# A chunked scan with an MLP behind it: decay loads, the order of the opening and the place of the long scan are changed

## Chip, core and metric

The kernel runs on one core of one Trainium2 chip. The core has a matrix engine (PE, its weight loads are shown as PEld), a vector engine (DVE), a scalar engine (ACT), GpSimd (POOL) and a queue engine (SyncE, SP) which here only issues DMAs; ACT can issue DMAs too. Each engine runs its own instructions in the order in which they were written. The metric is the device time of one execution in microseconds; less is better.

## What is computed

```python
log_a = np.log(np.clip(a, 1e-06, 1.0))
for c in range(nc):                       # chunks of the sequence
    cum = np.cumsum(la, axis=-1)
    L = np.exp(cum[..., :, None] - cum[..., None, :]) * causal
    y_intra = einsum('bhij,bhjd->bhid', einsum('bhin,bhjn->bhij', Cc, Bc) * L, xc)
    y_inter = einsum('bhin,bhnd->bhid', Cc, state) * exp(cum)
    state = exp(sum(la)) * state + sum_j Bc_j xc_j exp(cum_end - cum_j)
x = y.transpose(0, 2, 1, 3).reshape(3072, 256)
h = x @ w_in                              # 256 -> 2048
out = gelu_tanh(h) @ w_out                # 2048 -> 256
```

There are 4 batches of 8 heads with 768 tokens, 32 values a head and a state of 16; x, a, B and C come in as fp32, and so do the weights (2 MB each).

## The kernel before

The kernel takes chunks of 128 tokens, 6 to a batch, and works on **pairs** of chunks: pair u is 256 tokens, 12 pairs in all. Decays are never taken as logarithms: a backward running product of a (a scan on DVE) gives each token's decay to the end of its chunk, which scales B, and its reciprocal scales C. Steps are named by a letter and indices, and the names below are those of the order table.

- **Short decays**: `load_aq` brings the decays of chunks 0 to 3 of all batches as 128 rows of 128 into `aq_t`; `clipq`, `Rq` (scan, L331), `tpq` (32x32 turns, L342), `recip0` and `peq` follow on DVE. `mulb` and `mulc` (L416, L409) scale B and C of chunks 0 to 3 of batch 0, `tw` turns them on PE, `ew` copies them out of PSUM into `bh` and `ce`.
- **Long decays**: `load_a` brings all decays as 64 rows of 384 into `a_t`; `clip`, `R` (scan of 384, L331), `tp2`, `tp6` (turns), `recip1`, `recip`. Chunks 4 and 5 of batch 0 (pair 2) need `tp2`, `recip1`, `mul1`, `T1` (PE turns), `ce1`, `bh1`, `N1`, `bn1`; later batches need `tp6` and `recip`. `pe` and `pp` make `pend`, the decays of whole chunks.
- **A pair**: `G` (L595) makes the products of C and B in the PSUM tiles ga and gb, `M` (L605) masks them with the triangle on DVE. For pair 0 alone the half gb goes another way: `GE` copies it on ACT, `ME` (L616) masks it on POOL. `XX` and `XD` bring x of chunks 0 to 3 into rows and make the chunk's state, `S` (L676) carries the state on, `SP` (L683) spreads it. `Y` (L650, L659) makes y in PSUM tile yb, `yev` copies it to `xm`.
- **The MLP of a pair**: `s1.u.i` (L709, i from 0 to 7, four matmuls each) into one of two PSUM tiles hp, `gelu.u.i` on ACT, and `s2.u.k.q` (L727, four matmuls each, quarter q of w_out for chunk k) into PSUM tile o_ps; `oev` copies that out and `store` writes it. s1.u.0 and 1 need quarter 0 of w_in, 2 and 3 quarter 1, and so on.
- **Weights**: `load_wi.q` and `load_wo.q` bring a quarter (512 KB, fp32) each, `wi.q.k` and `wo.q.k` cast one half of a quarter to bf16 on POOL, DVE or ACT as the table says (L316, L318, L314).
- **Fillers**: `~n` stands for matmuls of zeros, n blocks of 128 columns, which keep PE running while it has nothing else.

Nothing is planned at run time. The string `ORDERED` lists every step; it is walked once, and each engine gets its instructions in that order (a letter behind the colon chooses the engine, A for ACT, D for DVE, P for POOL, S for SP). A step that waits holds everything that stands behind it on its engine. All loads but three go through SP's queue: two of the four `load_aq` and one `load_a` are issued by ACT.

Of the kernel before, what the change touches and what calls it, by code (L numbers as in the profile page):

```python
# [19 lines left out]
c_wz c_ident c_zero c_unp load_aq.2:A load_bc0.1 c_tri load_aq.1:S load_aq.3:S load_aq.0:A c_m8  # L20
c_sel c_warm c_m4 load_bc0.0 load_x4 clipq Rq tpq load_a.0:A load_a.1:S peq ~53 ppq pendq:A
load_wi.0 c_cz c_bmask recip0 mulc.0:D mulc.1:D mulb:P ~9 tw.1 tw.0 ew.0.0:D c_par ew.0.1:A tw.2
ew.0.2:A x4.1:D ~8 G.0 clip ew.1.0:A ew.1.1:A load_wi.1 M.0.0 GE.3 x4.0:P GE.2 load_wi.2 ~2 XX.0
XD.0 load_wo.0 xn.0:A ew.1.2:A SP.0 S.0.0 xn.1:A wi.0.0:A wi.0.1:A R ~13 G.1 S.0.1 load_wi.3 XX.1
load_bc1.0 xn.2:A ME.3:P ME.2:P pe Y.0 XD.1 pp yev.0.0.2:A S.1.0 load_wo.1 load_bc1.1 SP.1 S.1.1
load_wo.2 wi.1.1:P M.1.0 wi.2.0:P wo.0.0:D pend:A wo.0.1:P wi.2.1:P SP.2 wi.1.0:A M.1.1 s1.0.0
gelu.0.0 s1.0.1 gelu.0.1 xn.3:A wi.3.1:P s1.0.2+4 gelu.0.2 s1.0.3 s2.0.0.0.o load_wo.3 wo.1.0:P
gelu.0.3 load_bc.1.0 s1.0.4 wi.3.0:A s1.0.5 gelu.0.4 Y.1 tp2 mul1.0 gelu.0.5 yev.1.0.2:A s1.0.6
s1.0.7 gelu.0.6 load_x.2 tp6.0 load_bc.1.1 load_x.3 gelu.0.7 recip1 T1.0 s2.0.1.0.o s1.1.0 bh1:D N1
s1.1.1 wo.1.1:A tp6.3 s2.0.0.1.o wo.2.1:P gelu.1.0 gelu.1.1 mul1.1 tp6.2 T1.1 tp6.1 ce1.1:A ce1.0:A  # L30
wo.2.0:A bn1:D recip.1.4 s2.0.1.1.o s1.1.2 s1.1.3 gelu.1.2 wo.3.0:A wo.3.1:P G.2 gelu.1.3 s2.0.0.2.o
s2.0.1.2.o s2.0.0.3.o castx.2.None:P s2.0.1.3.o load_bc.2.1 M.2.0 mul.1.0 M.2.1 oev.1:A s1.1.4
s1.1.5 T.1.0 load_x.4 oev.0:A s2.1.0.0.o castx.3.None:P s2.1.0.1.o gelu.1.4 SP.3 D.2 gelu.1.5 s1.1.6
S.2.0 SP.4 load_x.5 E.1.0:A N.1 mul.1.1 bn.1:D gelu.1.6 s1.1.7 Y.2 s2.1.0.2.o T.1.1 gelu.1.7
yev.2.0.2:A s1.2.0 s1.2.1 gelu.2.0 E.1.1:D F.1 s2.1.0.3.o s1.2.2 gelu.2.1 gelu.2.2 D.3 load_bc.2.0
oev.2:D G.3 S.3.0 S.3.1 s2.1.1.0.o load_x.6 castx.4.None:P s1.2.3 gelu.2.3 s2.1.1.1.o s2.1.1.2.o
s1.2.4 M.3.1 M.3.0 gelu.2.4 SP.6 s2.1.1.3.o s1.2.5 oev.3:A gelu.2.5 D.4 Y.3 mul.2.1 S.4.0 G.4 s1.2.6
s2.2.0.0.o SP.7 castx.5.None:A yev.3.0.2:A gelu.2.6 S.4.1 s1.2.7 mul.2.0 s2.2.0.1.o s1.3.0
s2.2.0.2.o gelu.2.7 M.4.0 M.4.1 load_x.8 store_s.2.1 gelu.3.0 s1.3.1 s2.2.0.3.o s1.3.2 G.5 gelu.3.1
SP.8 gelu.3.2 store_s.2.0 D.5 Y.4 M.5.1 oev.4:A S.5.0 s1.3.3 s2.2.1.0.o s2.2.1.1.o gelu.3.3 s1.3.4  # L40
s1.3.5 s2.2.1.2.o yev.4.0.2:D s2.2.1.3.o SP.9 SP.10 gelu.3.4 gelu.3.5 s1.3.6 oev.5:A turn_s.2.1
s1.3.7 gelu.3.6 store.1 s2.3.0.0.o M.5.0 gelu.3.7 s2.3.0.1.o store.4 load_s.2 turn_s.2.0 load_x.7
# [23 lines left out]
gelu.10.3 s1.10.4 s1.10.5 oev.18:A gelu.10.4 s2.9.1.0.o s2.9.1.1.o gelu.10.5 s1.10.6 store.13
s1.10.7 s2.9.1.2.o s2.9.1.3.o gelu.10.6 gelu.10.7 s1.11.0 oev.19:A gelu.11.0 s1.11.1 s2.10.0.1.yb
s2.10.0.2.yb s2.10.0.3.yb gelu.11.1 oev.20:A store.20 store.18 s1.11.2 gelu.11.2 s1.11.3 s2.10.1.0.o
gelu.11.3 s2.10.1.1.o s1.11.4 s1.11.5 gelu.11.4 gelu.11.5 s2.10.1.2.o s2.11.0.0.yb s1.11.6 s1.11.7
gelu.11.6 s2.10.1.3.o s2.11.0.1.yb oev.21:D store.21 gelu.11.7 s2.11.0.2.yb s2.11.0.3.yb oev.22:A  # L70
store.22 store.19 s2.11.1.0.o s2.11.1.1.o s2.11.1.2.o s2.11.1.3.o oev.23:A store.23
# [891 lines left out]
```

## Time and profile before

| | us |
|---|---|
| runs | 116.67, 116.80, 116.95; median 116.8 |
| profiled execution, span (first to last instruction) | 115.1 |
| median less span, what lies around it | 1.7 |
| PE busy | 109.4 (95% of the span) |
| ACT busy | 75.1 (65%) |
| DVE busy | 68.7 (60%) |
| POOL busy | 15.1 (13%) |

The page gives no other time of the profiled execution than its span. Times in the views are microseconds from the start of the span. A row of the timeline reads: start, time from its start to the end of its last instruction, engine, line, operation, what is written and read, shapes, count, and in brackets the idle time of the engine just ahead with what ended it. Instructions of one engine overlap by some hundredths to tenths of a microsecond, so a duration is a little longer than the step from one start to the next.

### The profile page before, as it was taken

Reading aid. Unit: us, or ns where it says so; the run is one execution under the profiler, and the core shown is the slowest. Engines: PE = TensorE matmul, PEld = TensorE weight load, DVE = VectorE, ACT = ScalarE, POOL = GpSimd, SP = SyncE. Lnnn points to the kernel's source line nnn. Section 1 sums busy time; section 2 is a strip of 40 time slices with the busy share of each in tenths; the row PEclk is TensorE's granted clock in tenths of the full one; section 3 lists DMA queues with packets and bytes.
Section 4 is the critical chain, followed back from the end, with each engine's and each line's share of the span. In section 5 each row is a group of like instructions: output and inputs, shape, how many; then the busy total and the mean of one; then the engine's idle time right before and its main releaser. Section 6 shows DMA issues by size and latency. Waiting matters only on the chain.

```text
span 115.1 us, 3372 instructions
## 1 busy us (share of the span) xinstructions
PE 109.4 (95%) x1425; PEld 92.2 (80%) x1425; DVE 68.7 (60%) x135; ACT 75.1 (65%) x149; POOL 15.1 (13%) x32
## 2 busy tenths in 40 slices
PE   6999799999999999999999999999999999999990
PEld 2354578978877979799898998998989989999970
DVE  6688799998799989196966281546827421000100
ACT  3119889978657767657576486377766765685710
POOL 6564274122220000020002000000000000000000
PEclk9999999999999999999999999999999999999999
DMA  2999999949969828959478760000014014001132
GB/s 65 236 280 286 397 293 311 278 84 218 225 109 226 214 64 203 192 147 265 102 158 184 174 178 0 6 0 0 0 50 138 0 49 139 0 0 51 46 103 79
DMA packets 43006, 15.97 MB, mean 139 GB/s; under 512 B 36656, under 2 KB 41456, under 8 KB 42992
## 3 DMA queue, kind: packets, MB, share of 16 engines
q1 hardware_dynamic: 42848, 15.68, 53.9%
q8 instruction: 11, 0.18, 0.6%
q10 hardware_dynamic: 144, 0.08, 0.4%
q14 instruction: 3, 0.02, 0.1%
HBM read 11.04 MB, written 3.93 MB: 130 GB/s over the span
## 4 chain that ended last, share of the span: by engine, by line
PE 82%; DMA 8%; SPq 4%; POOL 1%; issue 1%; ACT 0%
PE hp L709 36%; PE o_ps L727 33%; DMA wf<-in_moe_w_out_dram 8%; PE yb L727 3%; PE ga L595 3%; PE yb L650 2%; PE yb L659 2%; SPq L190 1%; PE hp L628 1%; SPq L162 1%; SPq L159 1%; SPq L150 1%; POOL w_out_sb L316 1%; POOL w_in_sb L316 1%; SPq L183 1%
## 5 line engine op out<-in xcount | busy, mean ns | idle before, releaser
L713 ACT ACTIVATE gT<-hp 128x512 bf16<-128x512 f32 x96 | 53.3, 595 | 24.5 <-PE hp L709 24.0
L709 PE MATMUL hp<-xm,w_in_sb 128*128 128x256 bf16 x384 | 51.9, 273 | 0.5 <-ACT pend L314 0.3
L727 PE MATMUL o_ps<-w_out_sb,gT 128*128 128x256 bf16 x352 | 46.4, 273 | 0.0
L709 PEld LDWEIGHTS <-w_in_sb 128*128 128x128 bf16 x384 | 41.2, 114 | 3.2 <-issue 1.7
L727 PEld LDWEIGHTS <-gT 128*128 128x128 bf16 x384 | 37.0, 98 | 4.7 <-issue 0.8
L318 DVE COPY o_sb<-o_ps 128x256 f32<-128x256 f32 x7 | 3.0, 424 | 22.4 <-PE o_ps L727 18.4
L605 DVE TENSOR_TENSOR m<-ga,tri 128x1024 bf16<-128x1024 f32 x12 | 14.6, 1216 | 0.0
L605 DVE TENSOR_TENSOR m<-gb,tri 128x1024 bf16<-128x1024 f32 x11 | 13.4, 1219 | 0.5 <-PE gb L595 0.5
L697 PE MATMUL yb<-wz 128*128 128x512 bf16 (+2 forms) x24 | 8.2, 491 | 1.1 <-DVE warm L222 1.1
L314 ACT ACTIVATE o_sb<-o_ps 128x256 f32<-128x256 f32 x15 | 5.6, 382 | 4.1 <-PE o_ps L727 3.0
L683 DVE SCALAR_TENSOR_TENSOR sp_new<-s_new,pend,bmask 128x256 bf16<-128x256 f32 x17 | 8.0, 479 | 0.1
L316 POOL CAST x<-x_t 128x512 bf16<-128x512 f32 x5 | 3.2, 648 | 34.9 <-DMA x_t<-in_x_dram 22.9
L676 DVE SCALAR_TENSOR_TENSOR s_new<-s_new,pend,hp 128x64 f32<-128x64 f32 x13 | 3.6, 279 | 5.7 <-PE hp L628 5.5
L697 PEld LDWEIGHTS <-wz 128*128 128x128 bf16 x25 | 2.9, 126 | 5.0 <-issue 3.6
L659 PE MATMUL yb<-m,x 128*32 128x128 bf16 x192 | 6.1, 219 | 0.0
L650 PE MATMUL yb<-ce,sp_new 128*32 128x128 bf16 x160 | 5.3, 220 | 0.0
L595 PE MATMUL ga<-ce,bh 32*128 32x256 bf16 x48 | 4.7, 272 | 0.1
L314 ACT ACTIVATE xm<-yb 128x512 bf16<-128x512 f32 x8 | 4.8, 597 | 0.0
L595 PE MATMUL gb<-ce,bh 32*128 32x256 bf16 x48 | 4.7, 273 | 0.0
L727 PE MATMUL yb<-w_out_sb,gT 128*128 128x256 bf16 x32 | 4.1, 273 | 0.0
L659 PEld LDWEIGHTS <-x 128*32 128x32 bf16 x192 | 3.8, 97 | 0.4 <-issue 0.2
L650 PEld LDWEIGHTS <-sp_new 128*32 128x32 bf16 x160 | 3.0, 96 | 1.0 <-issue 1.0
(108 smaller groups left out, 78.4 us busy)
## 6 DMA issues: line engine op xcount, KB each, us to landing
out_dram<-o_sb SPq DMA_DIRECT2D x24, 128.0 KB, 2.0
x_t<-in_x_dram SPq DMA_DIRECT2D x20, 128.0 KB, 3.8
wf<-in_moe_w_in_dram SPq DMA_DIRECT2D x4, 512.0 KB, 8.3
wf<-in_moe_w_out_dram SPq DMA_DIRECT2D x4, 512.0 KB, 8.9
bc_t<-in_B_dram SPq DMA_DIRECT2D x3, 384.0 KB, 4.8
bc_t<-in_C_dram SPq DMA_DIRECT2D x3, 384.0 KB, 4.3
scr<-bc SPq DMA_DIRECT2D x4, 192.0 KB, 3.1
x_t<-in_x_dram SPq DMA_DIRECT2D x1, 512.0 KB, 4.8
```

The source lines that it names most:

```text
L314: nc.scalar.activation(o, i, AF.Copy)
L316: nc.gpsimd.tensor_copy(out=o, in_=i)
L595: nc.tensor.matmul(out=gbank(g)[:, 256 * k:256 * k + 256], lhsT=bh_of(2 * u + k)[gs], rhs=ce_of(2 * u + k)[gs], start=True, stop=True, til ...
L605: nc.vector.tensor_tensor(out=m_of(u)[:, 2 * i:2 * i + 2].rearrange("p g k e t -> p (g k e) t"), in0=gx[i].rearrange("p g (k t) -> p (g k) ...
L650: nc.tensor.matmul(out=y4[32 * j:32 * j + 32, k, w], lhsT=sp[:, 32 * h:32 * h + 32], rhs=ce_of(gc)[:, h % 2], start=first(j), stop=False, ...
L659: nc.tensor.matmul(out=y4[32 * j:32 * j + 32, k, w], lhsT=X16[u][:, k, 32 * h:32 * h + 32], rhs=m[:, h // 2, h % 2, :], start=first(j), st ...
L676: nc.vector.scalar_tensor_tensor(out=s_new, in0=state[("s", gc - 1)], scalar=pend_of(gc), in1=d, op0=ALU.mult, op1=ALU.add)
L683: nc.vector.scalar_tensor_tensor(out=sp_new.rearrange("p (g d) -> p g d", g=4), in0=(XN[0][:, H * D:H * D + 64] if gc == 0 else state[("s" ...
L697: nc.tensor.matmul(out=t[:, 0:m * 128], lhsT=wz, rhs=w3.to_broadcast([128, m, 128]), start=True, stop=True, skip_group_check=True)
L709: nc.tensor.matmul(out=hp[:, j * T:(j + 1) * T], lhsT=w_in_k[:, w, q, k], rhs=xm[:, w, u * T:(u + 1) * T], start=(w == 0), stop=(w == 1))
L713: nc.scalar.activation(gts[u][:, 2 * i:2 * i + 2], hps.pop((u, i)).rearrange("p (j t) -> p j t", j=2), AF.Gelu_apprx_tanh)
L727: nc.tensor.matmul(out=ops[gc], lhsT=gts[u][:, fi, k * Q:(k + 1) * Q], rhs=w_out_sb[:, fi, :], start=(fi == 0 and (u > 0 or k == 0)), stop ...
```

## The change

Loads: the four loads of the short decays become one, of 128 rows, first on SP (rows of other batches than 0, of which nothing is used later, now hold other values). B comes ahead of C, x directly behind C, then quarter 0 of w_in and the two loads of the long decays, all on SP. Quarter 0 of w_out comes ahead of quarter 2 of w_in.

```diff
-    def load_aq(i, eng):
-        (nc.scalar if eng == "ACT" else nc.sync).dma_start(out=aq_t[32 * i:32 * i + 32], in_=a_rows(i * Q, Q))
+    def load_aq(eng):
+        (nc.scalar if eng == "ACT" else nc.sync).dma_start(
+            out=aq_t, in_=bass.AP(tensor=a.tensor, offset=a.offset, ap=[[P4, 16], [S, H], [1, Q]]))
...
-    aq = [add("A", load_aq, i, alt="AS") for i in range(R4)]
+    aq = [add("S", load_aq, alt="S")]
```

The order of SP's first loads before (aq_t short decays, a_t long decays, bcf B and C, x_t x, wf a quarter of a weight):

```order
L150 DMA bcf_100<-in_C_dram 128x8x64
L159 DMA aq_t<-in_a_dram 32x128 x2
L150 DMA bcf_100<-in_B_dram 128x8x64
L183 DMA x_t<-in_x_dram 128x8x128
L162 DMA a_t<-in_a_dram 32x384
L190 DMA wf<-in_moe_w_in_dram 128x2x512 x3
L194 DMA wf<-in_moe_w_out_dram 128x1024
L190 DMA wf<-in_moe_w_in_dram 128x2x512
```

and of the change:

```order
L161 DMA aq_t<-in_a_dram 128x1x128
L152 DMA bcf_100<-in_B_dram 128x8x64
L152 DMA bcf_100<-in_C_dram 128x8x64
L186 DMA x_t<-in_x_dram 128x8x128
L193 DMA wf<-in_moe_w_in_dram 128x2x512
L165 DMA a_t<-in_a_dram 32x384 x2
L193 DMA wf<-in_moe_w_in_dram 128x2x512
L197 DMA wf<-in_moe_w_out_dram 128x1024
L193 DMA wf<-in_moe_w_in_dram 128x2x512 x2
```

x moved up by one place and the first weight quarter by two, and the quarters of w_in and w_out alternate differently. Further down, the x of pairs 3 and 4 and the store of chunk 0 now stand ahead of B and C of batch 2; the loads behind them keep their order.

Opening: the zero fill of `cz` moves from POOL to ACT, that of `unp` from DVE to POOL, and four copies into `unp` become one.

```diff
+        nc.scalar.activation(cz.rearrange("p e r h n -> p (e r) (h n)"),
+                             wz.rearrange("p (o n) -> p o n", o=1).to_broadcast([128, 2 * R4, H * N]), AF.Copy)
...
-        for r in range(R4):
-            nc.vector.tensor_copy(out=unp[:, r, :, r], in_=sub)
+        nc.vector.tensor_copy(out=diag, in_=sub.rearrange("p (o q) -> p o q", o=1).to_broadcast([128, R4, P4]))
```

The masks: pair 1 now goes the way of pair 0, so half of its mask leaves DVE for ACT and POOL. `s1.1.0` no longer depends on the last s1 of pair 0 (in the table it still stands directly behind it). An unused form of `SP` for POOL is added, and a single small matmul, `gate`, which waits for `tpq`.

```diff
+GEU = (0, 1)
...
-        if u:
+        if u not in GEU:
...
-                s.deps.append(s1.get((u - 1, NI - 1)))
+                s.deps.append(s1.get((u - 1, NI - 1)) if u > 1 else None)
...
+        elif w == "gate":
+            nc.tensor.matmul(out=yb[0:4, 0:1], lhsT=rt0[0][:, 0, 0:4], rhs=rt0[0][:, 0, 0:1],
+                             start=True, stop=True, skip_group_check=True)
```

The table: its first third is new, and from F.1 (batch 1) on it is nearly the old one. Two of its lines, before and after:

```diff
-S.0.0 xn.1:A wi.0.0:A wi.0.1:A R ~13 G.1 S.0.1 load_wi.3 XX.1
+wo.0.1:P wi.2.0:D wo.0.0:D clip R Y.1 yev.1.0.2:A s1.0.3 gelu.0.3 wi.2.1:P tp2
```

On DVE the place between the first masks and the turns of the long decays was this (r_t is the long scan, w_out_sb the cast of a weight half, m masks, sp_new and s_new states, pe the chunk decays):

```order
L331 SCALAR_TENSOR_TENSOR r_t<-ac,ends 64x384
L676 SCALAR_TENSOR_TENSOR s_new<-s_new,pendq,hp 128x64
L385 TENSOR_TENSOR pe_111<-ac,r_t 64x3
L387 TENSOR_TENSOR pe_112<-pe_111,m_117 64x24
L676 SCALAR_TENSOR_TENSOR s_new<-s_new,pendq,hp 128x64
L683 SCALAR_TENSOR_TENSOR sp_new<-s_new,pendq,bmask 128x256
L676 SCALAR_TENSOR_TENSOR s_new<-s_new,pendq,o_ps 128x64
L605 TENSOR_TENSOR m<-ga,tri 128x1024
L318 CAST w_out_sb<-wf 128x512
L683 SCALAR_TENSOR_TENSOR sp_new<-s_new,pendq,bmask 128x256
L605 TENSOR_TENSOR m<-gb,tri 128x1024
L342 STREAM_TRANSPOSE rt_126<-r_t 32x64 x4
```

and is now this, from pair 1's states on (bc0s is `mul1`; the two instructions of `ce1` come next):

```order
L329 CAST w_in_sb<-wf 128x512
L329 CAST w_out_sb<-wf 128x512
L339 TENSOR_SCALAR ac<-a_t 64x384
L342 SCALAR_TENSOR_TENSOR r_t<-ac,ends 64x384
L353 STREAM_TRANSPOSE rt_126<-r_t 32x64 x4
L353 STREAM_TRANSPOSE rt<-r_t 32x192 x2
L385 RECIPROCAL pt_128<-rt_126 128x16
L353 STREAM_TRANSPOSE rt<-r_t 32x192
L446 TENSOR_TENSOR bc0s_134<-bcf_101,pt_128 128x256
L446 TENSOR_TENSOR bc0s_134<-bcf_101,rt_126 128x256
L396 TENSOR_TENSOR pe_111<-ac,r_t 64x3
L398 TENSOR_TENSOR pe_112<-pe_111,m_117 64x24
```

The clip and the long scan now stand behind the casts of two weight halves (quarter 2 of w_in, quarter 0 of w_out). Before the turns the second half of pair 1's mask is gone from DVE; behind them `ce1` and one more weight cast have come from ACT and POOL, and `bh1` and `bn1` have gone to ACT.

On POOL the casts and masks after pair 0's mask read before:

```order
L616 AFFINE_SELECT m<-ge_140 128x512 x2
L316 CAST w_in_sb<-wf 128x512 x2
L316 CAST w_out_sb<-wf 128x512
L316 CAST w_in_sb<-wf 128x512 x2
L316 CAST w_out_sb<-wf 128x512 x3
```

and now:

```order
L627 AFFINE_SELECT m<-ge_140 128x512 x2
L327 CAST w_in_sb<-wf 128x512 x4
L627 AFFINE_SELECT m<-ge_141 128x512 x2
L327 CAST w_out_sb<-wf 128x512
L327 CAST w_in_sb<-wf 128x512 x3
L327 CAST w_out_sb<-wf 128x512 x4
```

POOL has 16 instructions here in place of 10: three more halves of w_in, one more of w_out, and pair 1's mask. The last two of the row x4 are both halves of quarter 3 of w_out, of which ACT had one before.

More of the change, by code (lines that the diff above doesn't have):

```diff
@@ L18 @@
 SCR = (2, 3)
+GEU = (0, 1)
 ORDERED = """
[L20 to L42, printed above, removed]
@@ L66 @@
[L66 to L71, printed above, removed]
+c_wz c_ident c_unp0:P c_bmask c_tri c_m8 c_sel c_m4 c_zero load_aq load_bc0.0 load_bc0.1 load_x4
@@ L226, in c_zero, with c_unp0 @@
         nc.vector.memset(ac[:, HS:HS + 1], 0.0)
-        nc.vector.memset(unp, 0.0)
+    def c_unp0(eng):
+        (nc.gpsimd if eng == "POOL" else nc.vector).memset(unp, 0.0)
     def c_warm():
@@ L297 @@
     xm = const.tile([128, 2, n_tokens], BF16, name="xm")
+    spf = [const.tile([128, 64], FP32, name=f"spf{i}") for i in range(2)]
     gx = [ps1.tile([128, 2, 512], FP32, name=f"g{i}") for i in "ab"]
@@ L679, in f_S, with f_SP @@
         state[("s", gc)] = s_new
-    def f_SP(gc):
+    def f_SP(gc, eng):
         sp_new = st.tile([128, 256], BF16, name="sp_new")
+        if eng == "POOL":
+            sc = spf[gc % 2]
+            nc.gpsimd.tensor_scalar(out=sc, in0=state[("s", gc)], scalar1=pend_of(gc + 1), scalar2=None, op0=ALU.mult)
+            nc.gpsimd.tensor_tensor(out=sp_new.rearrange("p (g d) -> p g d", g=4),
+                                    in0=sc.rearrange("p (o d) -> p o d", o=1).to_broadcast([128, 4, 64]),
+                                    in1=bmask.rearrange("p (g d) -> p g d", g=4), op=ALU.mult)
+            state[("sp", gc)] = sp_new
+            return
         nc.vector.scalar_tensor_tensor(
```

115 lines of the change are left out of this document (75 added, 40 removed).

## The prediction

> **What bounds the kernel now.** I read the chain of waits first: the page's shares of it by engine, then its pieces in order of time (start, length, engine and what is written).
>
> ```profile
> PE 82%; DMA 8%; SPq 4%; POOL 1%; issue 1%; ACT 0%
> ```
>
> ```profile
> 6.23 9.55 DMA wf<-in_moe_w_out_dram
> 15.83 0.87 POOL w_out_sb L316
> 16.70 0.76 POOL w_in_sb L316
> 17.51 0.96 PE hp L709 x7
> ...
> 112.11 0.38 ACT o_sb L314
> ```
>
> The program has two parts. From 17.51 to 112.11 PE is the chain and never pauses; behind it come one copy and one store. Ahead of 17.51 the chain is a weight load, its cast on POOL, and a second cast that stood behind it there. The second part is the same work in both kernels, in nearly the same order. So the time changes by how much earlier or later PE has done the same work at a place where both kernels have come together again, unless PE pauses after it. I take two such places from PE's timeline (start, length, engine, line, op, written and read, shapes, count):
>
> ```profile
> 14.18 1.03 PE L709 MATMUL hp<-xm,w_in_sb 128*128 128x256 bf16 x8 [0.28 <-ACT pend L314]
> ...
> 20.84 0.28 PE L463 MATMUL ga<-ident,bh 128*128 128x128 bf16 x2
> 20.95 0.60 PE L709 MATMUL hp<-xm,w_in_sb 128*128 128x256 bf16 x4
> 21.39 0.60 PE L727 MATMUL o_ps<-w_out_sb,gT 128*128 128x256 bf16 x4
> ...
> 23.67 1.92 PE L727 MATMUL o_ps<-w_out_sb,gT 128*128 128x256 bf16 x16
> ...
> 29.08 0.29 PE L650 MATMUL yb<-ce,sp_new 128*32 128x128 bf16 x8
> ```
>
> Four matmuls of an s1 or s2 take 0.44 (20.95 to 21.39), so 0.11 each. N1, two turns, takes 0.11 (20.84 to 20.95), so N.1, six turns, about 0.34. Place one is the end of pair 0's s2: 23.67 + 1.92 = 25.59. Ahead of it stand in both kernels all of pair 0, the first four s1 of pair 1, Y.1, T1 and G.2; only N1 follows it now instead. Place two is the start of Y.2, 29.08. The change has everything ahead of it but N.1, so being level there means 29.08 - 0.34 = 28.74.
>
> What holds PE up to these places are the weights. A cast that waited for a load shows when the load landed (ACT, then POOL):
>
> ```profile
> 11.78 1.15 ACT L314 ACTIVATE w_in_sb<-wf 128x512 bf16<-128x512 f32 x2 [0.19 <-DMA wf<-in_moe_w_in_dram]
> ...
> 23.87 0.63 ACT L314 ACTIVATE w_out_sb<-wf 128x512 bf16<-128x512 f32 x1
> ```
>
> ```profile
> 10.22 1.22 POOL L616 TENSOR_SCALAR_AFFINE_SELECT m<-ge 128x512 bf16<-128x512 bf16 x2 [1.71 <-ACT ge L610]
> 13.16 0.61 POOL L316 CAST w_in_sb<-wf 128x512 bf16<-128x512 f32 x1 [1.72 <-DMA wf<-in_moe_w_in_dram]
> ...
> 15.83 0.87 POOL L316 CAST w_out_sb<-wf 128x512 bf16<-128x512 f32 x1 [0.71 <-DMA wf<-in_moe_w_out_dram]
> ```
>
> Quarter 0 of w_in landed at 11.78, quarter 1 at 13.16, quarter 0 of w_out at 15.8, quarter 3 of w_out by 23.87. The last had its halves cast side by side on ACT and POOL, until 24.5. PE needs it for the last eight of the sixteen matmuls of 23.67, at about 24.6. It comes just in time: an earlier weight alone wins nothing here, a later one is paid in full.
>
> **The change: loads.** SP's timeline, then two stretches of one microsecond (PE, PEld, DVE, ACT, POOL busy, clock, DMA share, GB/s):
>
> ```profile
> 0.80 0.46 SPq L150 DMA_DIRECT2D bcf<-in_C_dram  x1
> 1.32 1.03 SPq L159 DMA_DIRECT2D aq_t<-in_a_dram  x2
> 2.39 0.42 SPq L150 DMA_DIRECT2D bcf<-in_B_dram  x1
> 2.86 0.58 SPq L183 DMA_DIRECT2D x_t<-in_x_dram  x1
> ```
>
> ```profile
> 3.00:4.00 1.00, 1.00 (x3) 0.29 (x2) 0.96 (x3) 0.23 (x2) 0.93 (x3) 1.00 0.89 174
> 23.00:24.00 1.00, 1.00 (x15) 0.57 (x14) 1.00 (x3) 1.00 (x3) 0.33 (x2) 1.00 0.20 40
> ```
>
> The bytes ahead of each landing are the same as before, with quarter 0 of w_out and quarter 2 of w_in (512 KB each) in exchanged places. So a quarter lands earlier only by what the stream starts earlier or runs denser. x was issued at 2.86. Now one short load (about 0.5, half of 1.03), B and C (0.42 and 0.46) stand ahead of it: 0.80 + 0.5 + 0.42 + 0.46 = 2.18, some 0.7 sooner. On the other side the first issue stays at 0.80, so the first byte comes no sooner, which makes nothing the lower end. Call the advance d. It lies between 0 and 0.7, and I take **d = 0.5**: nearer the upper end, since the weak stretch from 3 to 4 (174 GB/s), when small decay loads ran between C and B, should fill.
>
> **The short decays.** DVE's timeline, with the rows of the later parts too:
>
> ```profile
> 5.16 0.23 DVE L328 TENSOR_SCALAR acq<-aq_t 128x128 f32<-128x128 f32 x1 [0.89 <-DMA aq_t<-in_a_dram]
> ...
> 11.60 0.94 DVE L331 TENSOR_TENSOR_SCAN r_t<-ac,ends 64x384 f32<-64x384 f32 x1
> ...
> 15.80 0.43 DVE L318 CAST w_out_sb<-wf 128x512 bf16<-128x512 f32 x1
> 16.14 0.83 DVE L683 SCALAR_TENSOR_TENSOR sp_new<-s_new,pendq,bmask 128x256 bf16<-128x256 f32 x1
> ...
> 18.14 0.99 DVE L342 STREAM_TRANSPOSE rt<-r_t 32x64 f32<-32x64 f32 x4
> ...
> 28.18 0.48 DVE L683 SCALAR_TENSOR_TENSOR sp_new<-s_new,pend,bmask 128x256 bf16<-128x256 f32 x1
> ```
>
> DVE waited for the four loads until 5.16; the last of them was issued in the second half of 1.32 + 1.03, so it took some 3.2. One load issued at 0.80 should be there between 3 and 4, and the opening starts 1 to 2 earlier. What is late next is C, now third in the queue, and then quarter 0 of w_in: POOL casts both halves, 11.78 - d + 2 x 0.61 = 12.5, and PE's first s1 starts there instead of at 14.18. **These 1.7 are not in the sum**: PE meets the later weights anyway and spends them waiting.
>
> **Bound one, the last weight.** Quarter 3 of w_out lands at 23.87 - d. Both its halves now stand on POOL, one behind the other: 23.87 - d + 2 x 0.61 = 25.09 - d. Two of four matmuls of this s2 can run after the first half; two of it and four of its sister remain, 6 x 0.11 = 0.66. Place one is reached at 25.75 - d, and N1 (0.11) is still to come. Against 25.59 that is 0.27 - d; with d = 0.5 a **gain of 0.23**.
>
> **Bound two, DVE with the long scan late.** Quarter 2 of w_in lands where quarter 0 of w_out did, at 15.80 - d. Behind its cast on DVE stand a second cast (0.43 each), the clip of 384 (0.23 for 128 at 5.16; I take 0.35) and the scan, 0.94: 2.15, and 2.0 after overlaps. From the turns to the end of the last state spread ahead of Y.2 DVE took 28.18 + 0.48 - 18.14 = 10.5. Out of that stretch go the copies `bh1` and `bn1` to ACT; in come two of `ce1`, one cast of 0.43 and two tiny products of `pe`. The trace has `ce1` on ACT alone: between nothing more than the two copies and three casts more, 0 to 1.3; I take 0.5, one cast and the products, so 11.0. Y.2 can start at 15.80 - d + 2.0 + 11.0 = 28.8 - d; level is 28.74. Alone that would be a gain of 0.44 at d = 0.5, so bound one ends last, by 0.2.
>
> **Edits taken at nothing.** Pair 1's mask on POOL follows quarter 1's casts, 13.16 - d + 4 x 0.61 = 15.1. Y.1, which needs it, stood behind the group of 17.51 before, so it is free as long as POOL is less than 2 late; after that each microsecond is paid. The zero fill of `cz` on ACT, 1.2 by two halves of 1.15: ACT has nothing else until PE's first product, and if that cover went, mulc would wait. `unp` and the fillers lie ahead of the first s1, in the 1.7 that the sum leaves out; so does `gate`, behind which on PE only fillers and the first turns wait. The early store on SP waits for chunk 0's copy, just behind place one, and holds B and C of batch 2 and the x of pair 5; these are first used well behind 28.18, and a hold longer than that distance would be paid in full.
>
> **Rivals.** *The casts and DVE hinder each other* (slower). DVE cast from 15.80 and POOL from 15.83: POOL's cast took 0.87 in place of 0.61, and DVE's next spread, at 16.14 over the same cast, 0.83 in place of the 0.48 at 28.18. A meeting cost DVE 0.35 and POOL 0.26. The scan at 11.60 met nothing, since POOL stood still from 10.22 + 1.22 = 11.44 to 13.16. Now it runs, with two casts and the clip, while POOL has six casts nearly in a row: up to four meetings. DVE's bound becomes 28.8 - d + 0.35 k; from k = 1 it ends last, and with k = 3 it is 29.35, which against 28.74 is 0.6 slower: **117.4**. Against it: POOL also waits for landings in that stretch, so not each pair meets.
>
> [...]
>
> *The stream is not earlier*, d near 0.1. Then POOL's two casts in series are paid: 0.27 - 0.1 = 0.17 slower, **117.0**. For it speaks that the bytes are the same and the first issue too; against it x's earlier issue.
>
> *The stream is earlier by more*, d near 1. From 23 to 24 the DMA engines were 0.20 busy at 40 GB/s, while the last quarter was released only at 23.87: a few of the sixteen engines were late with their share. If they are not late again, both bounds move with d: 0.27 - 1.0 is a gain of 0.73, **116.0**. Against it: nothing in the change touches how a load is shared out.
>
> **How the numbers follow.** The median of the runs, 116.8, stands 1.7 above the span of 115.1; the shifts apply to both, so the forecast is 116.8 - 0.23 = **116.6**. A difference under about 0.2%, 0.23 us, can't be told from none. Chances: forecast 0.36, hindering 0.28, stream not earlier 0.16, stream much earlier 0.20. The forecast sits on the bound: 0.20 of its 0.36 go to faster, 0.16 to same. Hindering gives 0.26 slower and 0.02 same, the stream not earlier 0.05 slower and 0.11 same, the early stream 0.20 faster. Together faster 0.40, same 0.29, slower 0.31. The range reaches from a little beyond the early stream, 115.7, to three meetings with d a little smaller, 117.6.
>
> **What would show it.** Right: the first s1 at about 12.5, then pauses of PE in several places up to 24; quarter 3 of w_out released at about 23.4 with PE waiting for its second half; the spread ahead of Y.2 done by 28.3; no pause of PE behind that. Wrong: the scan or a cast longer by 0.3 than in these rows, Y.2 waiting for DVE, a pause of PE after Y.2, or weights released at times other than about 0.5 earlier.

## The result, and the profile after

The changed kernel took 118.73 us (median of 118.10, 118.63, 118.83, 119.36) beside 116.88 for the kernel before in the same round: a ratio of 1.0154, 95% interval 1.0113 to 1.0195. It is **slower by 1.5%**, 1.8 us. 116.6 was predicted, with a range from 115.7 to 117.6. Every ratio here leaves out executions that took over about 1.5% longer than the fastest of their kernel. The profiled execution has a span of 117.0, and its time was 118.83.

The chain of waits by engine (the page's line), and its longest pieces ahead of PE's part in order of time:

```profile
PE 78%; DMA 8%; SPq 5%; DVE 4%; issue 1%; ACT 0%
```

```profile
2.80 1.16 SPq L186
6.92 9.18 DMA wf<-in_moe_w_in_dram
17.60 1.34 DVE r_t L342
```

DVE, which had no share worth a name, now has 4%, and its longest piece is the long scan `r_t`. PE's timeline (start, length, ..., and in brackets its idle time with what ended it):

```profile
12.34 0.63 PE L728 MATMUL hp<-xm,w_in_sb 128*128 128x256 bf16 x4
...
16.61 0.30 PE L728 MATMUL hp<-xm,w_in_sb 128*128 128x256 bf16 x1 [0.59 <-DVE w_in_sb L329]
17.08 0.52 PE L728 MATMUL hp<-xm,w_in_sb 128*128 128x256 bf16 x3 [0.17 <-POOL w_in_sb L327]
...
19.39 1.06 PE L728 MATMUL hp<-xm,w_in_sb 128*128 128x256 bf16 x8 [0.49 <-POOL w_in_sb L327]
...
22.38 0.28 PE L454 MATMUL gb<-ident,bc0s 128*128 128x128 bf16 x2 [0.64 <-DVE bc0s L446]
...
24.02 0.28 PE L606 MATMUL ga<-ce,bh 32*128 32x256 bf16 x2
...
24.89 0.40 PE L404 MATMUL hp<-pe,selp 64*128 64x24 f32 x2
...
26.10 1.04 PE L746 MATMUL o_ps<-w_out_sb,gT 128*128 128x256 bf16 x8
...
30.40 0.30 PE L661 MATMUL yb<-ce,sp_new 128*32 128x128 bf16 x8
```

The first s1 starts at 12.34, 1.84 sooner than before. Then PE waits 0.76 for quarter 2 of w_in, 0.49 for quarter 3, and 0.64 at `T1.1` (22.38) for `mul1.1` on DVE. From there it doesn't pause. Place one, the end of pair 0's s2, is 26.10 + 1.04 = 27.14 in place of 25.59, and place two, the start of Y.2, is 30.40 in place of the level 28.74: 1.66 late. PE's last group of 16 matmuls is 1.65 late too (111.81 for 110.16), so nothing is lost in between; the rest of the 1.9 by which the span is longer lies behind PE's last matmul.

Most of the 1.66 was lost ahead of T1.1. In the kernel before, T1.0 and T1.1 started at 21.82; without T1.0 (0.11), N1 (0.11) and the one s1 (0.44) that no longer stand ahead of it, level there is 21.16, and 22.38 is 1.22 late. Another 0.33 is `pp`, the two fp32 matmuls at 24.89 (the step that follows starts at 25.22). In the kernel before it had stood ahead of the first s1:

```profile
13.49 0.40 PE L393 MATMUL hp<-pe,selp 64*128 64x24 f32 x2
```

It needs the long scan. With the scan late it had to move into the stretch in which PE never pauses, and there its time is paid. DVE and POOL ahead of T1.1 and up to Y.2:

```profile
16.12 0.43 DVE L329 CAST w_in_sb<-wf 128x512 bf16<-128x512 f32 x1 [1.15 <-DMA wf<-in_moe_w_in_dram]
16.46 0.83 DVE L329 CAST w_out_sb<-wf 128x512 bf16<-128x512 f32 x1
17.22 0.34 DVE L339 TENSOR_SCALAR ac<-a_t 64x384 f32<-64x384 f32 x1
17.60 1.33 DVE L342 TENSOR_TENSOR_SCAN r_t<-ac,ends 64x384 f32<-64x384 f32 x1
18.96 2.08 DVE L353 STREAM_TRANSPOSE rt<-r_t 32x64 f32<-32x64 f32 x6
...
21.89 0.43 DVE L446 TENSOR_TENSOR bc0s<-bcf,pt 128x256 bf16<-128x256 f32 x1
...
29.53 0.28 DVE L687 SCALAR_TENSOR_TENSOR s_new<-s_new,pend,hp 128x64 f32<-128x64 f32 x1 [0.47 <-PE hp L639]
29.84 0.48 DVE L702 SCALAR_TENSOR_TENSOR sp_new<-s_new,pend,bmask 128x256 bf16<-128x256 f32 x1
```

```profile
16.15 0.87 POOL L327 CAST w_in_sb<-wf 128x512 bf16<-128x512 f32 x1 [0.65 <-DMA wf<-in_moe_w_in_dram]
17.51 1.83 POOL L327 CAST w_in_sb<-wf 128x512 bf16<-128x512 f32 x2 [0.49 <-DMA wf<-in_moe_w_in_dram]
...
23.37 1.37 POOL L327 CAST w_out_sb<-wf 128x512 bf16<-128x512 f32 x2 [2.92 <-DMA wf<-in_moe_w_out_dram]
```

DVE waits 1.15 for quarter 2, which is there at 16.1. Then each thing that PE needs next, `T1.1` first, stands behind two casts, the clip and the scan. One cast took 0.83 for 0.43 and the scan 1.33 for 0.94, both beside a cast on POOL; POOL's two casts of quarter 3 took 1.83 where two alone take 1.17 to 1.22. DVE then has work until 30.32. The 0.47 idle in it, just ahead of the last state, are a wait for PE: at Y.2 DVE followed PE, and not PE DVE.

### The profile page after: what moved, and what is told of

It reads as the page before. It is cut to its first block, busy times and chain, and to the rows that moved or that the text cites. A ratio compares the mean times of both kernels' runs of the same rounds, so it can differ in the third digit from the quotient of the medians.

```text
span 117.0 us, 3374 instructions
## 1 busy us (share of the span) xinstructions
PE 109.1 (93%) x1425; PEld 91.4 (78%) x1425; DVE 69.8 (60%) x137; ACT 72.8 (62%) x141; POOL 19.2 (16%) x38
## 4 chain that ended last, share of the span: by engine, by line
PE 78%; DMA 8%; SPq 5%; DVE 4%; issue 1%; ACT 0%
PE hp L728 33%; PE o_ps L746 32%; DMA wf<-in_moe_w_in_dram 8%; PE yb L746 3%; PE ga L606 3%; PE yb L661 2%; PE yb L670 2%; DVE rt L353 2%; SPq L193 1%; DVE r_t L342 1%; PE hp L639 1%; SPq L186 1%; SPq L152 1%; SPq L165 1%; DVE w_out_sb L329 1%
## 5 line engine op out<-in xcount | busy, mean ns | idle before, releaser
L728 PE MATMUL hp<-xm,w_in_sb 128*128 128x256 bf16 x384 | 52.5, 273 | 1.9 <-POOL w_in_sb L327 0.7
L329 DVE COPY o_sb<-o_ps 128x256 f32<-128x256 f32 x7 | 3.0, 424 | 22.4 <-PE o_ps L746 18.4
L616 DVE TENSOR_TENSOR m<-gb,tri 128x1024 bf16<-128x1024 f32 x10 | 12.2, 1219 | 0.6 <-PE gb L606 0.5
L716 PE MATMUL yb<-wz 128*128 128x512 bf16 (+3 forms) x23 | 7.1, 443 | 1.1 <-DVE wz L222 1.1
L327 POOL CAST w_in_sb<-wf 128x512 bf16<-128x512 f32 x7 | 5.0, 743 | 1.6 <-DMA wf<-in_moe_w_in_dram 1.6
L716 PEld LDWEIGHTS <-wz 128*128 128x128 bf16 x23 | 2.3, 114 | 3.7 <-issue 2.0
L325 ACT ACTIVATE xm<-yb 128x512 bf16<-128x512 f32 x7 | 4.2, 598 | 1.0 <-PE yb L670 1.0
```

Source lines behind the costliest of these rows:

```text
L325: nc.scalar.activation(o, i, AF.Copy)
L327: nc.gpsimd.tensor_copy(out=o, in_=i)
L329: nc.vector.tensor_copy(out=o, in_=i)
L616: nc.vector.tensor_tensor(out=m_of(u)[:, 2 * i:2 * i + 2].rearrange("p g k e t -> p (g k e) t"), in0=gx[i].rearrange("p g (k t) -> p (g k) ...
L716: nc.tensor.matmul(out=t[:, 0:m * 128], lhsT=wz, rhs=w3.to_broadcast([128, m, 128]), start=True, stop=True, skip_group_check=True)
L728: nc.tensor.matmul(out=hp[:, j * T:(j + 1) * T], lhsT=w_in_k[:, w, q, k], rhs=xm[:, w, u * T:(u + 1) * T], start=(w == 0), stop=(w == 1))
```

## The experiments

Each ratio is to the kernel before, measured on the same chip in the same rounds. "T1.1" and "G.2" are the starts of these steps on PE in the profile, with PE's pause just ahead. The changed kernel's own numbers head the table. The last three columns come from one execution each, and these differ: the changed kernel's two profiles have G.2 at 24.02 and 22.87. The profile is of the shortest execution in runs 2, 5, 10, 14 and 15, of the longest in runs 3 and 4 and of the second longest in run 6.

| kernel | ratio, 95% interval | T1.1 (pause) | G.2 (pause) | span |
|---|---|---|---|---|
| changed | 1.0154, 1.0113 to 1.0195 | 22.38 (0.64) | 24.02 | 117.0 |
| 14 changed, again | 1.0150, 1.0111 to 1.0189 | 21.23 | 22.87 | 116.1 |
| 1 scan ahead of the casts | 1.0103, 1.0067 to 1.0138 | 21.43 | 23.28 | 116.2 |
| 2 quarter 3 on two engines | 1.0144, 1.0097 to 1.0191 | 21.52 (0.88) | 23.16 | 116.6 |
| 3 both | 1.0106, 1.0052 to 1.0161 | 23.59 | 25.22 | 118.2 |
| 4 quarter 2 of w_in first | 1.0086, 1.0051 to 1.0120 | 22.16 | 23.80 | 117.1 |
| 5 mul1.1 first | 1.0108, 1.0050 to 1.0165 | 20.73 | 23.25 (0.82) | 116.2 |
| 6 as 5, quarter 3 split | 1.0169, 1.0093 to 1.0245 | 20.63 | 23.72 (1.39) | 118.7 |
| 7 before, with the late scan | 1.0178, 1.0121 to 1.0236 | 24.40 | 25.93 | 117.7 |
| 8 a version put together early | 1.0220, 1.0159 to 1.0280 | 20.51 | 23.22 | 117.8 |
| 9 scan in the opening | 1.0044, 1.0003 to 1.0085 | 21.12 | 23.44 (0.48) | 116.4 |
| 10 as 5, ce1 on ACT | 1.0055, 1.0017 to 1.0092 | 20.58 | 22.21 | 115.7 |
| 11 9 and 10 | 1.0090, 1.0046 to 1.0134 | 21.18 | 22.80 | 116.2 |
| 12 short decays behind C | 1.0344, 1.0265 to 1.0423 | 25.00 (1.71) | 26.96 | 119.9 |
| 13 as 10, casts shared out | 1.0018, 0.9990 to 1.0047 | 19.88 | 21.51 | 114.8 |
| 15 as 13, long decays on ACT | 0.9977, 0.9949 to 1.0005 | 19.72 | 21.35 | 114.6 |

### Is it DVE's chain or the weights?

Run 1: the scan where DVE stood idle.

```diff
-S.1.1 s1.0.2 gelu.0.2 wo.0.1:P wi.2.0:D wo.0.0:D clip R Y.1
+S.1.1 s1.0.2 gelu.0.2 wo.0.1:P clip R wi.2.0:D wo.0.0:D Y.1
```

> The changed kernel took 118.7 us. On VectorE the clip and the long scan stand ahead of the casts of quarter 2 of w_in and quarter 0 of w_out, in the 1.15 us that VectorE stood idle there; nothing else is moved. Theory A (VectorE's chain from quarter 2's landing through the scan and the turns to mul1.1 sets PE's start on T1.1, and so the end): mul1.1 ends at least 1.0 sooner, PE's pause of 0.64 ahead of T1.1 is gone, time 118.0 to 118.2. Rival B (the pauses that PE makes for weights set the end, 0.59 + 0.17 at quarter 2 of w_in and 0.49 at quarter 3): quarter 2's cast comes up to 0.3 later, so the time is 118.7 to 119.0. Rival C (VectorE and GpSimd hinder each other): the scan, where GpSimd stands still, takes 0.94 in place of 1.33 and the casts behind it are longer instead; no gain beyond 0.2 of its own.

The pause at T1.1 is gone, and the ratio is 0.5% lower, as A said, though the two intervals overlap. But PE waits 1.28 for quarter 2's cast, which now stands behind the scan; and the scan took 1.25 here too, so C's free ground wasn't there.

Run 2: `wi.3.0:P` becomes `wi.3.0:A`, nothing else.

> One half of quarter 3 of w_in is cast on ACT in place of GpSimd, so both halves are done by about 18.5 in place of 19.3. A: PE's pause of 0.49 ahead of the seventh s1 of pair 0 goes, but T1.1 still waits for VectorE until 22.3, its pause grows by as much, time 118.7. B: the pause is won, time 118.2. C: GpSimd has one cast fewer beside the scan, the scan takes 1.0 to 1.2, T1.1 starts 0.2 sooner, 118.5.

This is the run that tells A from B. PE's timeline of this kernel:

```profile
18.32 1.04 PE L728 MATMUL hp<-xm,w_in_sb 128*128 128x256 bf16 x8
...
21.52 0.29 PE L454 MATMUL gb<-ident,bc0s 128*128 128x128 bf16 x2 [0.88 <-DVE bc0s L446]
```

The pause for quarter 3 is won (no bracket at 18.32), and given back at T1.1, where 0.64 has become 0.88. Quarter 2 was in time here, and still DVE was late:

```profile
15.30 0.83 DVE L329 CAST w_out_sb<-wf 128x512 bf16<-128x512 f32 x1
16.05 0.76 DVE L339 TENSOR_SCALAR ac<-a_t 64x384 f32<-64x384 f32 x1
16.84 1.24 DVE L342 TENSOR_TENSOR_SCAN r_t<-ac,ends 64x384 f32<-64x384 f32 x1
```

The cast, the clip and the scan each met POOL (0.43, 0.34 and 0.94 without). The ratio, 1.0144, can't be told from the changed kernel's. A weight that comes sooner wins nothing while DVE holds T1.1.

Run 3, both edits together:

> The scan early and quarter 3's halves on two engines together. A: both pauses are gone, since VectorE no longer holds T1.1 and then the weights come next: 117.4 to 117.8, more than the sum of the two alone. B: 118.2 to 118.5, as with the split alone. C: near 118.2.

A miss: 1.0106 is no better than run 1. In its profile PE waited 1.72 for the cast behind the scan, and a stretch of about 3.4 at half clock (0.50) followed, which the last section shows. That profile is of the longest of six executions (119.91), so it does not account for the ratio: the four with a mean clock of 0.997 or more took 117.75 to 118.56. Why the two edits don't add up stays open.

Run 4: loads and POOL's casts of quarter 2 ahead of quarter 0 of w_out.

```diff
-load_wi.1 load_wo.0 load_wi.2 load_wi.3
+load_wi.1 load_wi.2 load_wo.0 load_wi.3
...
-gelu.0.2 wo.0.1:P wi.2.0:D wo.0.0:D clip R ... wi.2.1:P tp2
+gelu.0.2 wi.2.1:P wo.0.1:P wi.2.0:D wo.0.0:D clip R ... tp2
```

> Quarter 2 of w_in is loaded ahead of quarter 0 of w_out, as in the kernel before, and GpSimd casts them in that order; VectorE's order is unchanged. A: quarter 2 is there by about 14.7, but VectorE's second cast and the scan behind it now wait for quarter 0 of w_out, landing near 16: T1.1 hardly moves, time 118.4 to 118.8. B: the pause of 0.76 for quarter 2 goes, time 118.0.

B's number, against A: 0.7% better. So the weights have a share of their own. T1.1 at 22.16 says little against A, since the profile is of the longest of eleven executions (118.97, median 118.10). PE's pauses didn't vanish in it, they moved: 0.41 to POOL's mask in Y.1, 0.43 to the cast of quarter 0 of w_out and 0.92 to quarter 3.

### Which part of DVE's chain

Run 5 moves the three wide turns behind what PE wants:

```diff
-tp2 s1.0.4 ... tp6.2 tp6.3 recip1 tp6.1 mul1.1 ... mul1.0 pe
+tp2 s1.0.4 ... recip1 mul1.1 ... mul1.0 tp6.2 tp6.3 tp6.1 pe
```

> The changed kernel with one thing moved on VectorE: the three wide turns of batches 1 to 3 (tp6.2, tp6.3, tp6.1, 1.53 together), which nothing on PE needs before the second s1 and s2 of pair 1, stand behind mul1.1 and mul1.0 in place of ahead of them. Loads, casts and the scan stay where they are. Theory A (VectorE's chain up to mul1.1 sets T1.1): mul1.1 ends 1.5 sooner after the same landing, PE's pause ahead of T1.1 (0.64, and 0.88 with the split) is gone, and the pauses for weights remain: 118.0 to 118.2. Rival B (only the pauses for weights count): 118.7.

The ratio is as A said, though its interval also holds the changed kernel's 1.0154; and the reason was too narrow. T1.1 came at 20.73 without a pause, and then PE stood still one step further on (PE, then DVE):

```profile
23.25 0.28 PE L606 MATMUL ga<-ce,bh 32*128 32x256 bf16 x2 [0.82 <-DVE ce L465]
```

```profile
20.31 1.56 DVE L353 STREAM_TRANSPOSE rt<-r_t 32x192 f32<-32x192 f32 x3
...
22.25 0.94 DVE L465 TENSOR_SCALAR ce<-gb,par 128x256 bf16<-128x256 bf16 x2
```

In runs 1, 2 and 5 G.2 starts at 23.28, 23.16 and 23.25. DVE does the same work in them, in three orders (that of run 2 is the changed kernel's), and its timelines list no idle time from the mask at 11.7 to 28.7. This suggests that the order doesn't matter, only the amount: **theory D**. That the three agree so closely is in part luck: the changed kernel's two profiles, also in the order of run 2, have 24.02 and 22.87. Run 6 adds the split of quarter 3.

> The same, with one half of quarter 3 of w_in cast on ACT. Alone that half won nothing, since PE's pause ahead of T1.1 grew by what was won. A: with T1.1 free it now wins its 0.3 to 0.5: 117.5 to 117.8. B: 118.2 or more, as without mul1.1 moved.

A miss: 1.0169. In the profile (120.43, mean clock 0.983) quarter 2 was late (DVE stood idle for 0.73 until 15.85), PE waited 1.39 for ce1 at G.2, and a stretch of about 3.4 at half clock (0.50) followed. D's reading holds (the pause moved to where DVE next hands over), the number doesn't.

Run 7 is the converse, the kernel before with nothing but the scan late:

```diff
-x4.1:D ~8 G.0 clip ew.1.0:A ... wi.0.1:A R ~13
+x4.1:D ~8 G.0 ew.1.0:A ... wi.0.1:A ~13
...
-wi.2.0:P wo.0.0:D pend:A wo.0.1:P
+wi.2.0:P wo.0.0:D clip R wo.0.1:P
```

(with `pe` behind `mul1.0`, and `pp` and `pend` behind the second gelu of pair 1.)

> The kernel before, with only the late scan of the change: clip and long scan stand on VectorE behind the cast of quarter 0 of w_out, pe behind mul1.0, and pp with its copy on PE and ACT behind the second gelu of pair 1. A: VectorE is 1.3 to 1.7 late from the spread SP.2 on, Y.1, T1.0 and T1.1 wait for it, and 1.0 to 1.5 are lost: 117.9 to 118.7 beside 116.9. B: the late scan is free, the loads and casts are those of before: 116.9 to 117.2.

It lost 1.8%, about as much as the whole change. DVE of this kernel:

```profile
16.02 0.43 DVE L318 CAST w_out_sb<-wf 128x512 bf16<-128x512 f32 x1 [0.37 <-DMA wf<-in_moe_w_out_dram]
16.36 0.76 DVE L328 TENSOR_SCALAR ac<-a_t 64x384 f32<-64x384 f32 x1
17.15 1.24 DVE L331 TENSOR_TENSOR_SCAN r_t<-ac,ends 64x384 f32<-64x384 f32 x1
```

Clip and scan take 0.35 + 0.94 where they stood before, with idle time around them. Here they take 2.0 of a full stretch, and PE waits 1.39 in Y.1 for the mask behind them. `pp` comes late with the scan here too: it stands at 24.07 on PE, just ahead of T1.1, and takes 0.33. So the late scan with what hangs on it is enough for a loss of this size. Whether it alone costs more than the whole change can't be told, as the intervals overlap, and the edit moves `pe`, `pp` and `pend` too.

Run 8 was an early attempt at a better order: quarter 2 first, clip and scan between the casts, four s1 of pair 1 moved up into PE's pauses, w_out's last quarter on ACT and POOL.

> A version built from the readings so far: the opening of the changed kernel; quarter 2 of w_in loaded ahead of quarter 0 of w_out and cast first; clip and scan behind that cast and ahead of w_out's; mul1.1 and mul1.0 right behind the first turns; four s1 of pair 1 moved ahead of the places where PE waited for weights; quarter 3's casts on ACT and GpSimd. If A and B are both parts of the loss: PE has no pause over 0.3 from 15.4 on until the last quarter of w_out, 116.0 to 116.6. If weights land later than quarter 3 of w_out did so far (23.3): 116.9.

A miss, the slowest of these but one. PE waited 0.62 for POOL's mask in Y.1, later 0.55 and 0.31 for ACT, and 0.69 for a spread on DVE in Y.2. It changed many things at once and shows only that this order has waits of its own.

### Taking work off DVE

Run 9 puts clip and scan in the opening, where DVE waited 0.71 for C, with the long decays loaded first by ACT.

```diff
-c_wz c_ident ... load_wi.0 load_a.1:S load_a.0:S load_wi.1 ... c_par mulb:P ... clip R
+load_a.0:A load_a.1:A c_wz c_ident ... load_wi.0 load_wi.1 ... c_par clip R mulb:P ...
```

> The changed kernel with clip and long scan in the opening on VectorE, ahead of mulc, where it stood idle for 0.71, and the two long decay loads issued first on ACT's queue; everything behind stays in its order. Theory D, formed from the first eight runs (VectorE has work without a gap from 11.7 to 28 whatever stands in which order, and PE's handover to it, at T1.1 or at G.2, comes when that work is done): the opening comes 0.6 to 0.9 later, 1.67 of work leaves the full stretch, G.2 starts at 22.4 to 22.9 in place of 24.0, time 117.2 to 118.0. Rival B (weights set the end): casts and loads are as before and PE comes later to them, 118.7. Rival E (the late scan only costs by its meetings with GpSimd, 0.4): 118.3.

The ratio is 1.0044: 1.1% better, 1.3 us, more than the 0.4 us of rival E, and B's 118.7 is out. But the edit also gives the long-decay loads to ACT, which by run 15 may be worth 0.4%; E with that would be about 1.008, just inside the interval. And with the clock taken into account (last section) the gain is about half. So the run leans to D and does not rule E out alone. G.2 missed D's 22.4 to 22.9: PE had no pause for weights here, but the first s1 came 0.91 later (13.25), and 0.48 of pause for ce1 stayed.

Run 10, on the order of run 5:

```diff
-gelu.0.7 ce1.1:D ce1.0:D s1.1.1 gelu.1.0 bh1:A s1.1.2 G.2 wo.2.0:D
+gelu.0.7 gelu.1.0 ce1.1:A ce1.0:A s1.1.1 bh1:A s1.1.2 G.2 wo.2.0:A
```

> The kernel with mul1.1 ahead of the wide turns, in which PE paused 0.82 at G.2 for VectorE's two ce1; these and one cast of quarter 2 of w_out now stand on ACT (behind the first gelu of pair 1), 1.37 less on VectorE. D: the pause at G.2 is gone or under 0.3, G.2 at 22.4 to 22.7, time 117.4 to 117.8. B: 118.3, as without it.

As D said: no pause at G.2, which starts at 22.21, a little sooner than D's 22.4 to 22.7, and 1.0055. That is 1% better than the changed kernel, clear of noise; run 5's 1.0108 is half a per cent more, with intervals that overlap. The work taken off DVE is 1.37; besides that, `gelu.1.0` stands earlier and one cast has gone to ACT.

Run 11, 9 and 10 together:

> Both: the scan in the opening, mul1.1 ahead of the wide turns, ce1 and the cast on ACT. D: VectorE is no longer the bound and PE is held by weights alone (0.6 to 1.2 of pauses before 20); 116.6 to 117.3, no more than the better of the two by 0.6. B: 118.3.

A miss, 1.0090. PE had two pauses only (0.37 and 0.25), and its first s1 came at 13.30 where run 10 had 12.21. Of these 1.09, 0.59 is left at G.2 (22.80 for 22.21): the later opening is paid in part. The intervals of the two runs overlap. Quarter 2 of w_out, with both halves on ACT, also came late.

Run 12, the load of the short decays behind B and C, tests the prediction's view that the opening is not in the sum:

> The changed kernel with the one load of the short decays behind B and C in place of first, so that the opening starts at 5 to 6 as in the kernel before. The prediction's step (the earlier opening is not in the sum, PE meets the weights anyway): 118.7, no change. D: VectorE's full stretch starts 1.5 to 2.2 later and its 1.15 idle ahead of quarter 2's cast is used up: G.2 0.4 to 1.0 later, 119.1 to 119.8.

Neither side said enough: 1.0344. The first s1 came at 15.26, 2.92 late, and PE's timeline goes on:

```profile
25.00 0.29 PE L454 MATMUL gb<-ident,bc0s 128*128 128x128 bf16 x2 [1.71 <-DVE bc0s L446]
```

2.62 of the 2.92 arrive at T1.1, though all weights it needs were long cast; the ratio is 1.9% above the changed kernel's, about 2.2 us. What the opening delays is DVE's full stretch, and most of that is paid.

### Both shares together

Run 13: as run 10, but POOL casts its half of quarter 2 ahead of w_out's, ACT casts one half of quarter 3, and quarter 2 of w_out is shared by ACT and POOL.

```diff
-gelu.0.2 wo.0.1:P wi.2.0:D ... wi.2.1:P tp2 ... wi.3.1:P wi.3.0:P
+gelu.0.2 wi.2.1:P wo.0.1:P wi.2.0:D ... tp2 ... wi.3.1:P wi.3.0:A
...
-wo.3.0:P wo.3.1:P castx.2.None:P ... wo.2.1:A gelu.1.1
+wo.2.1:P wo.3.0:P wo.3.1:P castx.2.None:P ... gelu.1.1
```

> The kernel with mul1.1 ahead of the wide turns and ce1 on ACT, in which the pauses left on PE were for casts; here GpSimd casts its half of quarter 2 of w_in ahead of that of quarter 0 of w_out, ACT one half of quarter 3, and the halves of quarter 2 of w_out stand on ACT and GpSimd. D and B together (VectorE's full stretch and the pauses for weights are the whole loss): PE runs from the first s1 at 12.3 to G.2 in 9.5 to 9.8, G.2 at 21.6 to 22.1, place one 0.4 to 0.9 sooner than in the kernel with ce1 on ACT, ratio to before 0.997 to 1.002. If something else is lost: ratio 1.005 or more.

G.2 at 21.51 and 1.0018, an interval that includes 1. The casts, of which one won nothing in run 2, now count. Together the two shares are the whole loss, as far as this can tell. How it splits is open. By the ratios DVE's work is about 1.0% (changed to run 10) and the pauses for casts about 0.4% (run 10 to 13, whose intervals overlap); but the casts alone, in run 4, won 0.7%, and the last section gives another reason.

> The changed kernel once more. D: with quarter 2 of w_in landing by 15 VectorE's stretch has no idle, G.2 at 23.2 to 23.4, span 116.2 to 116.5; with a landing after 16 again 117. Ratio to before 1.012 to 1.017, since the landing differs from run to run.

The changed kernel again: its ratio was 1.0150, and its profile has quarter 2 in time. DVE came to the cast at 15.32 without idling, G.2 was at 22.87 (D's 23.2 to 23.4 was missed), Y.2 at 29.25, the span 116.1. This was the shortest of six executions. T1.1, at 21.23, is level in it, and of the 0.5 that it is late at Y.2, 0.33 is `pp`. Runs 2 and 5, with DVE at the cast by 14.97 and 14.88, lost time too. So a late landing isn't the whole cause, it adds to it.

Run 15 moves `load_a.0` and `load_a.1` to ACT's queue, first of all.

> As e13, with the two long decay loads issued first on ACT's queue in place of behind quarter 0 of w_in on SP. If the issues on SP hold the weights, quarters 1 to 3 of w_in land 0.3 to 0.7 sooner; by D and B the casts are then no wait at all and the ratio is 0.001 to 0.004 below e13's. If the loads are limited by what the engines move, nothing changes, or the opening is 0.1 to 0.3 later.

0.9977, interval 0.9949 to 1.0005: level with the kernel before, perhaps 0.2% better. Quarter 3 of w_in landed 0.27 sooner than in run 13 (POOL's cast, which waited for it in both, began at 16.20 for 16.47); POOL, which had waited 0.21 for quarter 1, has no wait there, and for quarter 2 neither timeline lists one. In runs 13 and 15 Y.2 is about 0.9 ahead of level (27.91 and 27.76 beside 28.74), and the spans are only 0.3 and 0.5 shorter. Some 0.3 goes right behind Y.2, where N.1 and the turns of the next batch now stand (run 13):

```profile
29.18 0.51 PE L495 MATMUL gb<-ident,bc 128*128 128x128 bf16 x6 [0.20 <-DVE bc L486]
```

N.1's 0.34 stood ahead of place two before, so it is no gain to have it behind. PE's last group of 16 is 0.47 and 0.70 sooner than before (109.69 and 109.46), and the last 0.2 lies behind it.

## Why the prediction was wrong

- **The short decays**: the number is right, 12.34 for 12.5, the reason is not. The casts of quarter 0 were done by 11.75 (10.58 + 1.17), and the first s1 followed PE's own work without a pause.
- **"These 1.7 are not in the sum"**: wrong. Run 12 pays 2.62 of 2.92 at T1.1, run 11 0.59 of 1.09 at G.2. The view held only for PE and the weights. Behind the opening DVE has no slack, and its stretch starts with the opening.
- **d = 0.5**: not one number. The cast of quarter 0 of w_in began at 10.58 where it had been 11.78, that of quarter 3 of w_out at 23.37 for 23.87, but that of quarter 2 of w_in at 16.12, 0.3 later than the 15.80 of its place. x was issued at 2.80 and not 2.18, since each issue ahead took longer than in the rows it was taken from (0.69 for 0.5, 0.57 for 0.42 and 0.46).
- **Bound one**, the last weight: its terms held (POOL done at 23.37 + 1.37 = 24.74, forecast 24.6), but it bound nothing. PE came for that quarter at 26.10.
- **Bound two**: here the prediction failed. It had the right chain: quarter 2's release, two casts, clip, scan, turns. The step that failed is its sum, which took the release and the 2.0 behind it as undisturbed, with a margin of 0.44 to level: 15.3 + 2.0, so the turns at 17.3. Measured were 16.12 + 2.84, the turns at 18.96. Of this delay of 1.66, 0.8 is the release and 0.8 the two meetings with POOL (0.40 at the cast, 0.39 at the scan). The late release belongs to this execution: in runs 2, 5 and 14 DVE reached the cast at 14.97, 14.88 and 15.32 without idling, and the 2.0 came to 3.15, 3.24 and 2.47. So the meetings come each time, 0.5 to 1.2 in all, and the release only at times.
- **The handover was looked for too late**: the text named Y.2, where in the end DVE followed PE. PE had lost the time by T1.1, 8 us ahead, which waits on the same chain. By the rows before, the turns to the end of `mul1.1` take 3.46 (18.14 to 21.60), so the forecast 17.3 gives 20.8, in time for the level 21.16. From 18.96 it came to 22.32.
- **`pp` was not named**, and so stood at nothing. It cost 0.33 in PE's full stretch. No run moves it alone.
- **Edits at nothing**: the mask on POOL was done at 14.95, as said, and none of the zero fills, `gate` or the early store shows as a wait. But POOL, which took the mask, met DVE more often (its two halves took 1.61 for 1.22 beside DVE's spreads).
- **Rivals**: the first came true in kind (meetings of 0.40 and 0.39 where 0.35 was said). This profile has two of them, runs 2 and 5 have three, with Y.2 at 29.70 and 29.64 beside the rival's 29.35. Alone it gave 117.4. It fell short since `pp` and, in this profile, a late release came on top; the range held neither.

## What to carry to other kernels

Before a piece of work is moved later on an engine, ask whether it stood in idle time: clip and scan cost 1.3 in a gap, and up to 2.0 out of a stretch with none. When an engine is full from one point to another, moving steps within it mostly moves the pause of the engine that it feeds (0.64 at T1.1 became 0.82 at G.2 in run 5); the work has to leave it, and then the next limit shows. A step that only brings a full stretch forward can be worth most of what it brings forward (2.62 of 2.92 in run 12), even if the engine behind seems to wait for something else.
